# Idle matmuls, similarities and cluster rows moved in the prologue of a clustered-attention block on one Trainium2 core

## The chip, the cores and the metric

One NeuronCore of a Trainium2 chip runs the whole program. The metric is the device time of one execution in microseconds; several executions are timed and the median counts. One further execution is profiled.

The engines have these names in the rows: PE is TensorE (PEld its weight loads), DVE is VectorE, ACT is ScalarE, POOL is GpSimd, and SP is SyncE, whose queue issues every DMA of this kernel.

## What is computed

Batch 2, 8 heads, 768 positions, head size 64, 16 clusters per head. Queries and keys are put into the cluster whose centroid is most similar, a query sees only the keys of its own cluster, and two dense blocks follow.

```python
q_assign = np.argmax(np.einsum('bhsd,hcd->bhsc', q_n, c_n), axis=-1)
k_assign = np.argmax(np.einsum('bhsd,hcd->bhsc', k_n, c_n), axis=-1)
mask = q_assign[:, :, :, None] == k_assign[:, :, None, :]
scores = np.where(mask, scale * np.matmul(q, k.transpose(0, 1, 3, 2)), -1000000000.0)
scores = scores - np.max(scores, axis=-1, keepdims=True)
attn = np.exp(scores)
attn = attn / (np.sum(attn, axis=-1, keepdims=True) + 1e-09)
x = np.matmul(attn, v)          # then (B, S, H * D)
...
theta = x @ w_theta
y = w_tok_r @ (x * np.cos(theta)) + w_tok_i @ (x * np.sin(theta))
u = x + y
x = u + np.maximum(u @ w_ch, 0.0)
...
u = x + V.T @ (U.T @ x)
out = u + np.maximum(u @ w_ch1, 0.0) @ w_ch2
```

## The kernel before

**Tiles.** The 2 × 8 heads are worked on in eight pairs g = 0 to 7, two heads h per pair. A pair's queries and keys lie transposed, 128 × 768 (64 rows per head). For matmuls they are packed into tiles of 128 rows: `qp[s, h, w]` and `kp[s, h, w]`, in three sets s = g mod 3, with w = 0 and 1 for the high and the low parts of the numbers. Thirty-two of the 128 rows are free for extra terms: sixteen hold the **cluster rows**, a one-hot of the cluster on the query's side and 0 or -2**100 on the key's side, so that one matmul gives the score and its mask at once.

**Steps of a pair.**

- `split_hi`, `split_lo` (lines 186 to 194): hi on ACT, lo on POOL from the raw queries and keys; `pack` (line 215) copies them by DMA into the packed tiles.
- `assign_items` (line 115): the similarities `sims` on PE (line 121), then on DVE a transpose `s_t` (L124), the best similarity `mxc` (L128), four steps that make the one-hot `eqw` (L132 to L147) and a transpose back (L152).
- The cluster rows, in one of two ways. `mask_rows` (line 158): ACT makes `oh` (L161), and eight small DMAs copy it into the packed tiles. `mask_direct` (line 167): four matmuls turn the rows on PE (`oht`, L174), and ACT (L177, L179) or DVE (L181) copies them out. Pairs 0 and 1 use `mask_direct`, the later ones `mask_rows`.
- `max_pair(g, h, a)` (line 242): row maxima for two blocks of 128 queries, in three thirds of 512 columns, each with one bank `smax` (L251) and one reduction on DVE (L255). `max_join` joins the parts and splits them into two bf16 numbers, and `max_rows` (line 274) turns them into two more extra rows (`mrow`, L281; copied by ACT, L284).
- `scores_pair(g, h, a)` (line 294): transposed scores of two blocks of keys against all queries, in three thirds with one bank `st` each (L303); ACT takes the exp into `p` (L308).
- `pv` (line 312): products with V, four matmuls that the order lists and the trace book as eight, into two banks that are held until the pair's twelve are done; `sum_keys` (line 328): sums of the exps (`l`, L335).

**Order.** Nothing reorders the work: on every engine instructions run in the order of the code. PE's outputs go round a ring of eight banks of PSUM (`bank`, line 59), one of which, `hp`, is held for the idle matmuls of the prologue until its end (`give("hot")`). A step that needs a bank waits until the one before in it has been read.

The program has three parts. `prologue` (line 922) does the assignment and the cluster rows of pairs 0 and 1, all maxima of pair 0 and the scores of its head 0. `heat(n)` (line 927) issues n matmuls of a 128 × 512 tile of zeros whose result nobody reads. `attention` (line 829) loops over the pairs; in each of six places p it issues scores of pair g, then maxima of pair g + 1, then background work: `fill(t)` (line 811) takes items off the queue `bg` until their costs reach t, and conversions of weights when `bg` is empty. The splits of pair g + 2 and its one-hot steps stand in `bg`. PV products wait in `pvq` and are taken at p = 2 and p = 5. `mixer` (line 1016) is the rest.

SP's queue in the loop: at the start of pair g come V of pair g + 1, raw tiles of pair g + 3 and, from pair 1 on, weights; then the copies of `pack(g + 2)` as the splits come, then the eight copies of `mask_rows(g + 2)`.

Of the kernel before, what the change touches and what calls it, by code (L numbers as in the profile page):

```python
# [41 lines left out]
def tile_cluster_block(ctx: ExitStack, tc: tile.TileContext, qk, v, cent, wth, wr, wi, wch,  # L42
                       u_in, v_in, w1, w2, cst, out):
    nc = tc.nc
# [14 lines left out]
    def bank(name, keep=None):  # L59
        i = ring.popleft()  # L60
        if keep is None:
            ring.append(i)
        else:
            kept.setdefault(keep, []).append(i)
        return pp.tile([P, 512], F32, tag=f"bank{i}", name=name)
# [8 lines left out]
    def f32(ap):  # L74
        return ap.bitcast(F32)
# [91 lines left out]
    def mask_direct(g, h, eng):  # L167
        x = XROW[h]
        r = slice(x, x + 16)
        for i in range(2):  # L170
            for hf in range(2):
                o = 32 * (2 * i + hf) + 16 * h
                ps = bank("oht")
                nc.tensor.matmul(out=ps[r, :HALF], lhsT=identb[:, o:o + 16], rhs=onehots[g], start=True, stop=True)  # L174
                src, dst = ps[r, :HALF], (qp, kp)[i][g % SETS, h, 0][r, cols(hf)]
                if i == 0:
                    nc.scalar.activation(out=dst, in_=src, func=AF.Copy)  # L177
                elif eng is nc.scalar:
                    nc.scalar.activation(out=dst, in_=src, func=AF.Identity, scale=BIG, bias=kmul[r, 2:3])  # L179
                else:  # L180
                    eng.tensor_scalar(dst, src, BIG, BIG, op0=ALU.mult, op1=ALU.subtract)  # L181
# [9 lines left out]
    def split_lo(g, i, eng):  # L191
        t = slot(f"lo{g}_{i}", F32R)
        eng.tensor_tensor(t, raw[g, i], f32(hl[g, i, 0]), op=ALU.subtract)
        hl[g, i, 1] = t
# [44 lines left out]
    mx_t = {}  # L239
    THIRDS = [[(0, 0, 512)], [(0, 512, 256), (1, 0, 256)], [(1, 256, 512)]]  # L240

    def max_pair(g, h, a):

        s = g % SETS
        if a == 0:
            mx_t[g, h] = small.tile([P, 2 * NT], F32, tag="mx12", name="mx12")
        o = 2 * a
        for part in THIRDS:
            ps, c = bank("smax"), 0
            for j, k0, w in part:  # L250
                nc.tensor.matmul(out=ps[:, c:c + w], lhsT=qp[s, h, 0][:, (a + j) * P:(a + j + 1) * P],  # L251
                                 rhs=kp[s, h, 0][:, k0:k0 + w], start=True, stop=True)
                c += w
            n = len(part)
            nc.vector.tensor_reduce(mx_t[g, h][:, o:o + n], ps.rearrange("p (n w) -> p n w", n=n), axis=AX.X, op=ALU.max)  # L255
            o += n

    def max_join(g, h, act=False):
        mx = small.tile([P, NT], F32, tag="mx", name="mx")
# [34 lines left out]
    def scores_pair(g, h, a):  # L294

        s = g % SETS
        for kt in (a, a + 1):
            pt[g, h, kt] = slot(f"p{h}")
        for part in THIRDS:
            ps, c = bank("st"), 0  # L300
            for j, q0, n in part:
                for w in range(2):
                    nc.tensor.matmul(out=ps[:, c:c + n], lhsT=kp[s, h, w][:, (a + j) * P:(a + j + 1) * P],  # L303
                                     rhs=qp[s, h, w][:, q0:q0 + n], start=(w == 0), stop=(w == 1))
                c += n
            c = 0
            for j, q0, n in part:
                nc.scalar.activation(out=pt[g, h, a + j][:, q0:q0 + n], in_=ps[:, c:c + n], func=AF.Exp,  # L308
                                     scale=float(D) ** -0.5)
                c += n  # L310
# [496 lines left out]
    assign = {}  # L807
# [21 lines left out]
    def attention():  # L829


        ORDER = [(0, 0), (0, 2), (0, 4), (1, 0), (1, 2), (1, 4)]
        BURST = (2, 5)
        pvq = deque()
        held[0] = True

        def next_pv():
            g, kt, hf = pvq.popleft()
            pv(g, kt, hf)
            if kt == NT - 1 and hf:  # L840
                pv_out(g)

        for g in range(NG):
            nxt = g + 1 < NG
            if nxt:
                load_v(g + 1)
            if g + 2 < NG:
                bg.extend(split_items(g + 2, nc.gpsimd))
                bg.extend(assign.pop(g + 2))
            if g + 3 < NG:  # L850
                for i in range(2):
                    load_raw(g + 3, i)
            if g == 1:
                conv_load.extend(weigh_in(wth, NP * DM, wth_t))
                conv_start()
            if g == 2:
                tok = [c for p in zip(weigh_in(wr, NT * S, wr_t), weigh_in(wi, NT * S, wi_t)) for c in p]
                conv_load.extend(tok[:6])
                conv_start()
                late = tok[6:]  # L860
            if g == 6:
                conv_load.extend(late)
                conv_start()
            if not nxt:
                for t in range(NP):
                    bg.append((1., lambda t=t: split_x(0, t, nc.gpsimd)))
            order = [(1, 0), None, (1, 2), None, (1, 4), None] if g == 0 else ORDER
            for p in range(NT):
                ready = len(pvq)
                if order[p]:  # L870
                    h, a = order[p]
                    scores_pair(g, h, a)
                    if h:
                        pvq.extend((g, kt, hf) for kt in (a, a + 1) for hf in range(2))
                if g == 0 and p < 2:
                    mask_direct(1, p, nc.scalar if p else nc.vector)
                if nxt:
                    max_pair(g + 1, p // 3, 2 * p % 6)
                    if p % 3 == 2:
                        max_join(g + 1, p // 3)  # L880

                while conv_after:
                    conv_after.popleft()()
                if p == 3 and g + 2 < NG:
                    mask_rows(g + 2)
                if g > 0 and p == 5:
                    bg.appendleft((.95, lambda: norm_x(g - 1)))
                    bg.appendleft((.97, lambda: spread(g - 1)))
                fill(2. if not nxt else 4.8 if p in BURST else .3)
                if not nxt:  # L890
                    if p == 0:
                        sum_keys(g - 1, 1)
                    if p == 2:
                        max_rows(g, 1)
                    if p == 5:
                        sum_keys(g, 0)
                    for _ in range(min(ready, (2, 2, 2, 0, 4, 4)[p])):
                        next_pv()
                elif p in BURST:
                    if p == 2 and g > 0:  # L900
                        max_rows(g, 1)
                        sum_keys(g - 1, 1)
                    if p == 5:
                        max_rows(g + 1, 0)
                        sum_keys(g, 0)
                    for _ in range(min(ready, 6)):
                        next_pv()
                    if p == 5 and g + 3 < NG:
                        (_, sims), *assign[g + 3] = assign_items(g + 3)
                        sims()  # L910
                if g > 0 and p == 2:
                    row_sums(g - 1)
            while bg:
                fill(.5)
        held[0] = False
        while len(pvq) > 1:
            next_pv()
        nc.scalar.activation(out=warm, in_=warm, func=AF.Sin)
        next_pv()
        sum_keys(NG - 1, 1)  # L920

    def prologue():
# [4 lines left out]
        def heat(n):  # L927

            for _ in range(n):
                nc.tensor.matmul(out=hp, lhsT=hot[:, :P], rhs=hot[:, :512], start=True, stop=True)  # L930
# [34 lines left out]
        def run(items):  # L965
            for it in items:
                it[1]()

        its, its1 = assign_items(0), assign_items(1)
        for i in range(2):  # L970
            split_hi(0, i)
        split_lo(0, 0, nc.gpsimd)
# [8 lines left out]
        init_packs(1, nc.gpsimd)  # L981
        heat(14)
        run(its[1:])
        run(its1[:1])
        mask_direct(0, 0, nc.vector)
        mask_direct(0, 1, nc.scalar)
        split_lo(0, 1, nc.gpsimd)
        pack_low(0, (0, 1))
        for i in range(2):
# [2 lines left out]
        pack_direct(1, 0)  # L992
        pack(1, main=(1,))
        pack_low(1, (0,))
        for a in (0, 2, 4):
            max_pair(0, 0, a)
        max_join(0, 0, act=True)
        max_pair(0, 1, 0)
        max_pair(0, 1, 2)
        max_rows(0, 0)  # L1000
        init_packs(2, nc.gpsimd)
        scores_pair(0, 0, 0)
        max_pair(0, 1, 4)
        max_join(0, 1)
        run(its1[1:])
        scores_pair(0, 0, 2)
        heat(2)
        scores_pair(0, 0, 4)
        heat(2)
        max_rows(0, 1)  # L1010
        its2 = assign_items(2)
        run(its2[:4])
        assign[2] = its2[4:]
        give("hot")

    def mixer():
# [165 lines left out]
```

## Time and profile before

| what | value |
|---|---|
| median of 3 executions | 683.65 us (682.72 to 684.89) |
| the profiled execution | 684.69 us |
| its span, first to last instruction | 682.9 us |
| mean granted clock of TensorE | 0.994 |
| PE busy | 669.9 us, 98% of the span |
| DVE, ACT, POOL busy | 66%, 51%, 40% |

The span is what the profile shows; 1.8 us of the execution lie outside it. A busy time is the union of an engine's instructions, and a matmul is booked until its modelled end, so that PE's share holds more than the time in which it streams. The granted clock is the part of TensorE's full speed that the chip allows at the moment.

### The profile page before, as it was taken

To read this page: it belongs to the slowest core of one execution; us is meant where nothing else is said; L and a number is where in the kernel's file an instruction comes from. 1 tells how busy PE (TensorE), PEld (TensorE's weight loads), DVE (VectorE), ACT (ScalarE), POOL (GpSimd) and SP (SyncE) were. 2 spreads that over 40 slices of the span, in tenths; PEclk is the share of its full clock that TensorE was granted. 3 is DMA by queue.
4 is the path that set the end of the run, shared out by engine and by line. 5 is a ranking of instruction groups with operands and counts; after the bars stand their busy time and mean duration, and the time that the engine had idled before them with its cause. 6 is when DMAs were issued, how large, how long until landed. Compare 5 with 4: busy or idle time off the path is not lost.

```text
span 682.9 us, 11925 instructions
## 1 busy us (share of the span) xinstructions
PE 669.9 (98%) x4611; PEld 570.3 (84%) x4612; DVE 453.5 (66%) x800; ACT 350.5 (51%) x713; POOL 270.2 (40%) x273
## 2 busy tenths in 40 slices
PE   8999999999999999999999999999999999999997
PEld 3567766755765599999999998798899999999997
DVE  6887887898787367547375445877386766765554
ACT  7657656665776554456464344434454543543221
POOL 9423223133235324113223102466666566646221
PEclk9899999999999999999999999999999999999999
DMA  6768688576622102003110210212221212200013
GB/s 206 206 146 254 167 239 230 158 195 159 178 94 87 54 1 78 1 1 108 47 42 12 78 32 1 79 61 78 76 78 56 71 61 78 63 0 1 1 47 138
DMA packets 21784, 62.55 MB, mean 92 GB/s; under 512 B 4224, under 2 KB 7296, under 8 KB 21728
## 3 DMA queue, kind: packets, MB, share of 16 engines
q1 hardware_dynamic: 21728, 61.80, 30.9%
q8 instruction: 36, 0.59, 0.3%
q14 instruction: 20, 0.16, 0.1%
HBM read 40.35 MB, written 3.15 MB: 64 GB/s over the span
## 4 chain that ended last, share of the span: by engine, by line
PE 89%; DVE 6%; ACT 4%; issue 1%; DMA 0%; SPq 0%; DVEq 0%; ACTq 0%
PE y L562 15%; PE acc L796 15%; PE q L744 13%; PE pv L316 9%; PE st L303 8%; PE l L335 5%; PE th L520 5%; PE acc L717 5%; PE g L698 4%; PE h L582 4%; PE smax L251 3%; DVE mx L255 2%; ACT p L308 2%; PE sims L121 1%; DVE xT L646 1%; ACT hi L188 1%
## 5 line engine op out<-in xcount | busy, mean ns | idle before, releaser
L255 DVE TENSOR_REDUCE mx<-smax 128x1 f32<-128x512 f32 x144 | 89.6, 682 | 21.9 <-PE smax L251 21.9
L401 POOL TENSOR_TENSOR wl<-cv,wh 128x768 fp32r<-128x768 f32 (+1 forms) x33 | 57.9, 1754 | 115.2 <-ACT wh L397 93.7
L308 ACT ACTIVATE p<-st 128x512 f32<-128x512 f32 x192 | 79.0, 513 | 44.2 <-PE st L303 43.3
L796 PE MATMUL acc<-g,wh 128*128 128x384 f32 x384 | 97.5, 334 | 0.0
L562 PE MATMUL y<-wh,z 128*128 128x384 f32 x384 | 87.6, 340 | 0.3 <-ACT z L540 0.3
L758 POOL TENSOR_TENSOR g<-sum,g 128x384 fp32r<-128x384 f32 x48 | 53.3, 1113 | 80.7 <-ACT g L757 75.5
L752 DVE TENSOR_TENSOR xT<-acc,xT 128x384 f32<-128x384 f32 x96 | 53.3, 556 | 45.0 <-PE acc L796 44.8
L303 PE MATMUL st<-qp,kp 128*128 128x256 f32 (+1 forms) x384 | 79.4, 349 | 0.4 <-ACT qp L284 0.2
L303 PEld LDWEIGHTS st<-qp,kp 128*128 128x128 f32 x384 | 58.3, 192 | 18.9 <-issue 8.5
L796 PEld LDWEIGHTS acc<-g,wh 128*128 128x128 f32 x384 | 69.3, 188 | 0.0
L562 PEld LDWEIGHTS y<-wh,z 128*128 128x128 f32 x384 | 66.9, 188 | 0.5 <-ACT z L540 0.5
L316 PE MATMUL pv<-p,v 128*32 128x384 f32 x768 | 66.2, 486 | 0.0
L796 PE MATMUL acc<-g,wl 128*128 128x384 f32 x192 | 64.1, 334 | 0.0
L752 DVE TENSOR_TENSOR sum<-q,sum 128x384 f32<-128x384 f32 x84 | 45.5, 554 | 27.2 <-PE q L744 22.0
L756 ACT ACTIVATE sum<-sum 128x384 f32<-128x384 f32 x48 | 25.1, 523 | 67.5 <-DVE sum L752 67.5
L316 PEld LDWEIGHTS pv<-p,v 128*32 128x32 f32 x768 | 31.6, 110 | 29.4 <-issue 20.7
L546 POOL TENSOR_TENSOR z<-tht,z 128x256 fp32r<-128x256 f32 x24 | 19.3, 802 | 87.6 <-ACT z L540 87.5
L392 DVE SCALAR_TENSOR_TENSOR cv<-cv,st 128x768 int32<-128x768 int32 (+3 forms) x47 | 46.8, 995 | 3.1 <-ACT cv L385 2.6
L562 PE MATMUL y<-wl,z 128*128 128x384 f32 x192 | 48.8, 335 | 0.0
L251 PE MATMUL smax<-kp,qp 128*128 128x512 f32 x192 | 44.2, 349 | 3.0 <-ACT qp L177 1.9
L251 PEld LDWEIGHTS smax<-kp,qp 128*128 128x128 f32 x192 | 33.0, 191 | 12.7 <-issue 2.9
L385 ACT ACTIVATE cv<-st 128x768 f32<-128x768 f32 (+3 forms) x47 | 38.3, 815 | 10.3 <-POOL wl L401 4.1
(170 smaller groups left out, 1450.7 us busy)
## 6 DMA issues: line engine op xcount, KB each, us to landing
st<-in_w_dram SPq DMA_DIRECT2D x17, 512.0 KB, 3.4
st<-in_w_dram SPq DMA_DIRECT2D x10, 768.0 KB, 4.1
raw<-in_qk_dram SPq DMA_DIRECT2D x16, 384.0 KB, 4.5
qp<-hi SPq DMA_DIRECT2D x26, 192.0 KB, 2.9
st<-in_wr_dram SPq DMA_DIRECT2D x6, 768.0 KB, 4.6
st<-in_wi_dram SPq DMA_DIRECT2D x6, 768.0 KB, 4.3
kp<-hi SPq DMA_DIRECT2D x32, 96.0 KB, 3.1
qp<-lo SPq DMA_DIRECT2D x32, 96.0 KB, 2.7
```

What stands on the lines that cost most here:

```text
L251: nc.tensor.matmul(out=ps[:, c:c + w], lhsT=qp[s, h, 0][:, (a + j) * P:(a + j + 1) * P], rhs=kp[s, h, 0][:, k0:k0 + w], start=True, stop=True)
L255: nc.vector.tensor_reduce(mx_t[g, h][:, o:o + n], ps.rearrange("p (n w) -> p n w", n=n), axis=AX.X, op=ALU.max)
L303: nc.tensor.matmul(out=ps[:, c:c + n], lhsT=kp[s, h, w][:, (a + j) * P:(a + j + 1) * P], rhs=qp[s, h, w][:, q0:q0 + n], start=(w == 0), st ...
L308: nc.scalar.activation(out=pt[g, h, a + j][:, q0:q0 + n], in_=ps[:, c:c + n], func=AF.Exp, scale=float(D) ** -0.5)
L316: nc.tensor.matmul(out=pvt[g][hf][r:r + 32, :HALF], lhsT=v_t[g][:, kt, r:r + 32], rhs=pt[g, r // 64, kt][:, cols(hf)], start=(kt == 0), st ...
L392: nc.vector.scalar_tensor_tensor(t, t, 3, self.lw, op0=ALU.logical_shift_left, op1=ALU.bitwise_or)
L401: nc.gpsimd.tensor_tensor(t[:, :c.w], c.t, f32(c.hi[:, :c.w]), op=ALU.subtract)
L562: nc.tensor.matmul(out=yps[u, j][hf][:, :HALF], lhsT=lhs, rhs=w[st][e][:, hf * HALF:(hf + 1) * HALF], start=(st == 0 and n == 0), stop=(st ...
L744: nc.tensor.matmul(out=ps[:, :HALF], lhsT=w[a][:, j * P:(j + 1) * P], rhs=u_block(self.b, y, e, j), start=(n == 0), stop=(n == 5))
L752: nc.vector.tensor_tensor(out, ps[:, :HALF], x, op=ALU.add)
L758: nc.gpsimd.tensor_tensor(t[:, 1], r, f32(t[:, 0]), op=ALU.subtract)
L796: nc.tensor.matmul(out=ps[:, :HALF], lhsT=wv[a], rhs=self.g[i, hf][:, x], start=(m == 0), stop=(m == 5))
```

## The change

In the prologue: idle matmuls are added (three behind pair 0's cluster rows, one behind each third of four of pair 0's six groups of maxima, six before pair 1's first cluster rows) and two times two are removed. The similarities of pair 1 move from before pair 0's cluster rows to behind its first group of maxima, with `s_t` and `mxc`. The similarities of pair 2 move ahead of `max_rows(0, 1)`, and its step L132 moves out of the prologue into the background of the loop. Pair 1's cluster rows move from the loop into the prologue, one head before and one behind the scores (0, 1, 0), which come with them.

In the loop: pair 0's remaining scores are issued at p = 1 and p = 3, its first four PV products stand in the queue from the start, and at p = 5 of pair 0 four instead of six are taken.

```diff
-    def max_pair(g, h, a):
+    def max_pair(g, h, a, warmer=None):
...
             nc.vector.tensor_reduce(mx_t[g, h][:, o:o + n], ps.rearrange("p (n w) -> p n w", n=n), axis=AX.X, op=ALU.max)
             o += n
+            if warmer:
+                warmer(1)
...
-        pvq = deque()
+        pvq = deque((0, kt, hf) for kt in (0, 1) for hf in range(2))
...
-            order = [(1, 0), None, (1, 2), None, (1, 4), None] if g == 0 else ORDER
+            order = [None, (1, 2), None, (1, 4), None, None] if g == 0 else ORDER
...
-                if g == 0 and p < 2:
-                    mask_direct(1, p, nc.scalar if p else nc.vector)
...
-                    for _ in range(min(ready, 6)):
+                    for _ in range(min(ready, 6 if g else 4)):
...
-        its, its1 = assign_items(0), assign_items(1)
+        its, its1, its2 = assign_items(0), assign_items(1), assign_items(2)
...
         run(its[1:])
-        run(its1[:1])
         mask_direct(0, 0, nc.vector)
         mask_direct(0, 1, nc.scalar)
+        heat(3)
...
-        for a in (0, 2, 4):
-            max_pair(0, 0, a)
+        max_pair(0, 0, 0)
+        run(its1[:2])
+        max_pair(0, 0, 2, heat)
+        max_pair(0, 0, 4, heat)
         max_join(0, 0, act=True)
-        max_pair(0, 1, 0)
-        max_pair(0, 1, 2)
+        max_pair(0, 1, 0, heat)
+        max_pair(0, 1, 2, heat)
         max_rows(0, 0)
         init_packs(2, nc.gpsimd)
         scores_pair(0, 0, 0)
         max_pair(0, 1, 4)
         max_join(0, 1)
-        run(its1[1:])
+        run(its1[2:])
         scores_pair(0, 0, 2)
-        heat(2)
         scores_pair(0, 0, 4)
-        heat(2)
+        run(its2[:2])
         max_rows(0, 1)
-        its2 = assign_items(2)
-        run(its2[:4])
-        assign[2] = its2[4:]
+        heat(6)
+        mask_direct(1, 0, nc.vector)
+        scores_pair(0, 1, 0)
+        mask_direct(1, 1, nc.scalar)
+        assign[2] = its2[3:]
         give("hot")
```

**Around the first maxima.** DVE before, from the transpose of pair 0's one-hot (`eqw`) on; `kp_87` is the key tile of set 0, head 0, w = 0:

```order
L152 STREAM_TRANSPOSE eqw<-eqw 128x384
L124 STREAM_TRANSPOSE s_t<-sims 128x384
L181 TENSOR_SCALAR kp_87<-oht 16x384 x2
L255 TENSOR_REDUCE mx_288<-smax 128x1
L255 TENSOR_REDUCE mx_288<-smax 128x2
```

and DVE now:

```order
L152 STREAM_TRANSPOSE eqw<-eqw 128x384
L181 TENSOR_SCALAR kp_87<-oht 16x384 x2
L255 TENSOR_REDUCE mx_284<-smax 128x1
L255 TENSOR_REDUCE mx_284<-smax 128x2
L255 TENSOR_REDUCE mx_284<-smax 128x1
L124 STREAM_TRANSPOSE s_t<-sims 128x384
L128 TENSOR_REDUCE mxc<-s_t 128x24
L255 TENSOR_REDUCE mx_284<-smax 128x1
```

Pair 1's `s_t` went from ahead of the cluster-row copy to behind the first three reductions, and `mxc`, which stood behind all of pair 0's maxima, came along. PE now, in the same place (`raw_0_120` and `raw_1_122` are pair 1's raw tiles, `qp_85` is the query tile beside `kp_87`):

```order
L251 MATMUL smax<-kp_87,qp_85 128x512
L121 MATMUL sims<-raw_0_120,cblk 32x384
L121 MATMUL sims<-raw_1_122,cblk 32x384
L121 MATMUL sims<-raw_0_120,cblk 32x384
L121 MATMUL sims<-raw_1_122,cblk 32x384
L251 MATMUL smax<-kp_87,qp_85 128x512
L930 LDWEIGHTS hot
L930 MATMUL hot<-hot 128x512
L251 MATMUL smax<-kp_87,qp_85 128x256 x2
L930 LDWEIGHTS hot
L930 MATMUL hot<-hot 128x512
```

Before, the maxima stood there one behind the other.

**At the end of the prologue, on ACT.** `p` are exps, `qp_93` belongs to pair 1's head 0, `qp_97` and `kp_99` to its head 1, `hi_0` and `hi_1` are the splits of pair 2. Before:

```order
L308 ACTIVATE p_468<-st 128x512
L177 ACTIVATE qp_93<-oht 16x384 x2
L188 ACTIVATE hi_0_507<-raw_0_194 128x768
L188 ACTIVATE hi_1_509<-raw_1_196 128x768
L177 ACTIVATE qp_97<-oht 16x384 x2
L179 ACTIVATE kp_99<-oht,kmul 16x384 x2
L308 ACTIVATE p_556<-st 128x512
```

Now:

```order
L310 ACTIVATE p_489<-st 128x512
L177 ACTIVATE qp_97<-oht 16x384 x2
L179 ACTIVATE kp_99<-oht,kmul 16x384 x2
L188 ACTIVATE hi_0_534<-raw_0_194 128x768
L188 ACTIVATE hi_1_536<-raw_1_196 128x768
L310 ACTIVATE p_560<-st 128x512
```

The copies of head 1's cluster rows went ahead of the splits (those of head 0 now stand ahead of the exps `p_488` and `p_489`).

**In the loop, on ACT.** Pair 2, first half, from the conversion `wh` behind the first exps on; `hi_0`, `hi_1` are the splits of pair 4. Before:

```order
L397 ACTIVATE wh<-cv 128x768
L308 ACTIVATE p_1109<-st 128x512
L308 ACTIVATE p_1109<-st 128x256
L308 ACTIVATE p_1110<-st 128x256
L308 ACTIVATE p_1110<-st 128x512
L188 ACTIVATE hi_0_1136<-raw_0_728 128x768
L188 ACTIVATE hi_1_1138<-raw_1_730 128x768
L308 ACTIVATE p_1162<-st 128x512
```

Now:

```order
L310 ACTIVATE p_1153<-st 128x512
L310 ACTIVATE p_1153<-st 128x256
L310 ACTIVATE p_1154<-st 128x256
L310 ACTIVATE p_1154<-st 128x512
L188 ACTIVATE hi_0_1185<-raw_0_737 128x768
L188 ACTIVATE hi_1_1187<-raw_1_739 128x768
L286 ACTIVATE qp_106<-mrow 2x384 x2
```

The splits went from between the second and the third exps to behind the third. The same holds for pair 3; in pair 1 they went from behind the first exps to behind the third, and in pairs 4 and 5 from between the second and third to directly behind `wh`, ahead of the second.

## Rows read from the trace of the kernel before

**Rows 1.** The page, section 2: granted clock in 40 equal slices of the span.

```profile
PEclk9899999999999999999999999999999999999999
```

**Rows 2.** Busy time of each engine by stretch; then granted clock, DMA share, GB/s.

```profile
core 0: us, PE busy (x) PEld busy (x) DVE busy (x) ACT busy (x) POOL busy (x), PEclk, DMA share, GB/s
14.53:21.22 6.69, 5.63 (x21) 3.26 (x21) 5.87 (x12) 4.99 (x9) 5.95 (x5) 0.91 0.88 273
21.22:26.80 5.58, 5.29 (x20) 3.92 (x20) 4.58 (x8) 2.82 (x6) 4.44 (x7) 0.50 0.96 207
...
33.17:37.63 4.46, 3.26 (x17) 1.75 (x16) 3.00 (x7) 4.39 (x10) 1.77 (x1) 1.00 0.16 36
```

**Rows 3.** Timeline, 10 to 40 us, all engines: start, length, engine, what, count, wait before.

```profile
9.67 2.14 PE L930 MATMUL hot<-hot 128*128 128x512 bf16 x9
...
11.07 0.58 DVE L152 STREAM_TRANSPOSE eqw<-eqw 128x384 bf16<-128x384 bf16 x1
...
12.66 0.58 DVE L124 STREAM_TRANSPOSE s_t<-sims 128x384 f32<-128x384 f32 x1 [1.02 <-PE sims L121]
...
13.28 1.04 DVE L181 TENSOR_SCALAR kp<-oht 16x384 fp32r<-16x384 f32 x2
...
14.53 6.24 PE L251 MATMUL smax<-kp,qp 128*128 128x512 f32 x20 [0.74 <-ACT qp L177]
...
15.04 5.47 DVE L255 TENSOR_REDUCE mx<-smax 128x1 f32<-128x512 f32 x9 [0.72 <-PE smax L251]
...
21.22 0.49 PE L281 MATMUL mrow<-identb,m 128*2 128x128 bf16 x6 [0.45 <-DVE m L271]
...
26.37 1.76 PE L303 MATMUL st<-qp,kp 128*128 128x512 f32 x8
...
30.92 0.58 DVE L152 STREAM_TRANSPOSE eqw<-eqw 128x384 bf16<-128x384 bf16 x1
...
33.17 0.82 PE L174 MATMUL oht<-eqw,identb 128*16 128x384 bf16 x4
...
34.88 1.58 ACT L188 ACTIVATE hi<-raw 128x768 fp32r<-128x768 f32 x2
...
35.18 0.93 PE L251 MATMUL smax<-kp,qp 128*128 128x512 f32 x4 [1.20 <-ACT qp L177]
...
35.85 3.74 POOL L193 TENSOR_TENSOR lo<-raw,hi 128x768 fp32r<-128x768 f32 x2 [10.14 <-issue]
```

**Rows 4.** Timeline of PE alone, 27 to 53.4 us.

```profile
39.91 2.79 PE L316 MATMUL pv<-p,v 128*32 128x384 f32 x32
...
53.31 0.50 PE L303 MATMUL st<-qp,kp 128*128 128x512 f32 x1
```

**Rows 5.** Timeline of SP's queue, 53.9 to 80 us: start and length of the issues.

```profile
54.00 1.38 SPq L376 DMA_DIRECT2D st<-in_wth_dram  x3
...
67.81 0.54 SPq L213 DMA_DIRECT2D qp<-lo  x1
...
76.61 0.54 SPq L213 DMA_DIRECT2D kp<-oh  x1
```

**Rows 6.** DMA issues, 53.9 to 79.7 us: count, KB each, median us to landing.

```profile
st<-in_wth_dram SPq DMA_DIRECT2D x1, 512.0 KB, 12.8
...
kp<-oh SPq DMA_DIRECT2D x4, 24.0 KB, 1.9
```

**Rows 7.** Timeline of PE alone, 77.2 to 90.6 us.

```profile
78.82 0.86 PE L251 MATMUL smax<-kp,qp 128*128 128x512 f32 x4
...
83.01 0.85 PE L251 MATMUL smax<-kp,qp 128*128 128x512 f32 x4
...
84.51 2.14 PE L335 MATMUL l<-p,ones 128*32 128x384 f32 x24 [0.21 <-ACT p L308]
```

**Rows 8.** Timeline of ACT alone, 77.2 to 90.6 us.

```profile
81.79 1.64 ACT L188 ACTIVATE hi<-raw 128x768 fp32r<-128x768 f32 x2
...
83.26 1.69 ACT L308 ACTIVATE p<-st 128x512 f32<-128x512 f32 x4
```

## The prediction

> **What bounds the kernel now.** I read the granted clock first, then the prologue in order of time on all engines, then PE through the loop of pair 0, then the DMA queue, and last one later pair on PE and ACT. TensorE is the engine that sets the time, and nearly the only stretch in which it neither works densely nor runs at full speed is the prologue. The clock line shows one loss: of its forty digits the second is 8, and all others are 9 [rows 1]. The stretches show where: 0.91 of full clock while the first maxima are taken (14.53 to 21.22 us), 0.50 in the 5.58 us behind them, 1.00 again later [rows 2]. 0.50 is the lower of TensorE's two levels, 1.2 GHz. In the stretch ahead of the fall PE is booked 5.63 of 6.69 us, but that is 20 matmuls of the maxima and little else; it is DVE that works through, one third of a pair of row maxima every 0.6 us (9 in 5.47 us) [rows 3]. So PE waits for banks there and the matmuls come in small groups.
>
> The other idle place is the wait for the second pair's cluster rows: the maxima at 35.18 wait 1.20 us, and PE is busy only 3.26 of the 4.46 us around it [rows 2, 3].
>
> **The change, part by part.** Each step is dated against the profiled execution.
>
> *Similarities of pair 1 out of the way.* Their transpose s_t stands on DVE at 12.66 to 13.24, ahead of the cluster-row copy kp at 13.28 (1.04 us for two) [rows 3]. Without sims and s_t the turned rows can follow eqw (ready at 11.65) directly: cluster matmuls at 11.7, kp copied by about 13.35, first maxima at 13.55 in place of 14.53. The three idle matmuls put in here cost nothing as long as they stay under that copy; at 0.24 us each (9 in 2.14 us) [rows 3] they end at about 13.55 too. If the copy came earlier they would be the wait. Gain 0.95.
>
> *It comes back on DVE.* The first nine reductions now have s_t and mxc among them, 0.6 us each. Ready for mrow: 13.55 + 0.5 + 9 × 0.6 + 1.2 + 0.8 for joining and splitting, about 21.45, against 21.22 [rows 3]: 0.25 later. So the first scores start no earlier.
>
> *The idle matmuls.* Twelve of 0.24 us are put where PE waits for DVE: per third 0.24 of maxima and 0.24 idle work against DVE's 0.6. They fit; what they are for is the clock. Taken as held at 1.00, the scores and maxima from 21.45 on run at full rate; the next limit is DVE's reductions, which release the banks. The second scores pair then starts at about 25.3 in place of 26.37 [rows 3]. Gain 1.1.
>
> The Trainium skill, page "TensorE: Matmul & The Clock Gate", section "Why this matters for your kernels", says that what drops the clock in mid-kernel is idle gaps between bursts of matmuls, and means gaps far longer than any in this stretch; by that rule the clock would not have fallen here, and more matmuls could not mend it. The row on the clock says that it fell, so the row decides here; what the rule would give is rival 2.
>
> *Cluster rows of pair 1 before head 1's scores.* DVE ends the chain of pair 1 at about 30.05 in place of 31.50, six idle matmuls end at about 30.3 (0.2 us too late, the one place where they cost), cluster rows, scores (0,1,0) and the other cluster rows follow without a gap, and pair 1's maxima start at about 33.05 instead of 35.18 [rows 3], with four cluster matmuls already done (0.8 us of PE as in the row at 33.17).
>
> *The loop of pair 0.* It took from 35.18 to 53.31 [rows 3, 4] with PE dense. It loses one scores pair and the cluster rows to the prologue and passes 16 of its PV matmuls (half of the 32 at 39.91 in 2.79 us [rows 4], so 1.35 us) on to pair 1. But it is now thin on PE and meets two others. ACT: the two splits hi (1.58 us [rows 3]) stand behind all four cluster copies and ahead of the exps of scores (0,1,2), whose banks the third maxima and the PV products need. From 35.0 the splits run to 36.5, the first bank is read at 37.15 and the last at 38.1; PE would want them 0.6 and 0.3 us before: 0.9 of waiting. DVE: 14 of the 18 reductions must be done before `l` gets a bank. From 33.55 these are 14 × 0.6 us, and the five steps of pair 2's one-hot (some 0.55 each, as L152 [rows 3]) with a join stand among them, 3.4 us: 45.4, where PE could be 1.2 us before. Behind it come 2.0 for `l`, 2.6 for four PV products and 0.65 for sims: 50.6 for the first scores of pair 1, 2.7 earlier, and 1.35 of it is owed later. Net 1.35, and nearly 1.7 at the first scores of pair 2, since ACT no longer splits between two exps of pair 1.
>
> *Where that ends.* The first maxima of pair 3 (78.82 [rows 7]) need four small copies of cluster rows, the last issued at 76.61 on SP [rows 5] and landing 1.9 us later [rows 6], at 78.5. That is 0.3 us ahead of PE. SP issues in order: behind the weight loads (issued 54.00 to 55.38) its copies stop until the third weight load lands (12.8 us after issue [rows 6], so 67.8), and from 67.81 on it issues without a break, twenty copies of some 0.6 us [rows 5]. Backwards this hangs on the split of pair 2, hi at 34.88 on ACT and lo at 35.85 on POOL (3.74 us) [rows 3]. The change puts cluster copies ahead of hi and brings all else forward; I get 34.9 to 35.05, no earlier. So SP's queue is not moved, PE may run 1.7 us ahead and waits for 78.5 to 78.7. What is left of the gain is 0.1 us (bounds: none of it, if hi is a little later; all of 1.7, if the copies did not decide).
>
> *The shifted background.* Because pair 2's one-hot has a step more to do in the loop, the splits of later pairs move on ACT. In pairs 2 and 3 they stood between the second and third exps (hi at 81.79, p at 83.26 [rows 8]) and made l at 84.51 wait [rows 7]; now they come behind. Worth 0.2 (the wait that the row names) to 0.8 (84.51 less the end of a 0.7 us group begun at 83.01 [rows 7]); I take 0.55 each, because mrow stands between the two and takes a part of the larger. In pairs 4 and 5 they come ahead of the second exps, where the scores of the third pair then wait for banks: 0 to 1.6 us lost, the whole 1.64 of the two splits; I take 0.4 each, since PE's two groups take 2.1 us (78.82 to 83.01 is two pairs) against ACT's 1.69 [rows 7, 8], which gives back 0.4 a time, and part of the wait was there before. Later pairs and the conversions behind only change places; I put 0 ± 0.5 on them.
>
> The sum: 0.1 + 2 × 0.55 − 2 × 0.4 = 0.4 us saved. The profiled execution took 684.69, its span 682.9 and 1.8 around it, 1.0 more than the median of 683.65; the sum makes 684.3 of it, and by the same difference **683.2** of the median.
>
> **The rivals.** About 0.3% (2.05 us) is what a measurement of this kernel can tell from no change.
>
> 1. *The copies do not decide* (SP comes earlier, or the reshuffled background gains in more places than it loses). Then the 1.7 us stay, with 1.1 from pairs 2 and 3, less 0.8: 681.6; without the loss in pairs 4 and 5, 680.8. For it: the slack is a few tenths of a microsecond, and such an issue row varies by that. Against it: twenty issues in a row without a gap. 0.22.
>
> 2. *The idle matmuls do not hold the clock.* PE then meets 21.45 to 27 at half rate as now, 0.25 later than now and with the extra matmuls in the way, hi comes about 1.1 later, and the copies with it: 0.8 lost at pair 3, 0.3 won behind: 684.1. For it: the page's rule above; against it: PE will be issuing in every gap. 0.10.
>
> 3. *The clock falls in the new wait*, at the first maxima of pair 3. PE arrives some 1.6 us early and stands still at a place where it is the bound from then on. The fall in the prologue lasted at least the 5.58 us of [rows 2] at half rate, which in a dense stretch is 2.8 us of work: 686.1. It decides from a wait longer than any that the clock has survived so far, 1.20 us at 35.18 [rows 3]. Against it: PE was dense on both sides of that one, as it is here. 0.07.
>
> 4. *The splits of pair 2 come late.* Each microsecond by which hi starts behind 35.2 moves the copies of pair 3 by as much. From about 2.3 us on the kernel is slower by more than can be told from nothing: 685.8. 0.07, since what ACT waits for ahead of that place comes 2 us forward.
>
> My forecast has 0.54; its own range is 682.2 to 684.4.
>
> **How the numbers follow.** Of rival 1 some two thirds lie over 0.3%, and a little of the forecast's reordering: faster 0.18. Rivals 3 and 4 make slower 0.14. The rest is within 0.3%: 0.68. The range of 681.0 to 685.2 holds the forecast, rival 2 and most of rival 1, and leaves out rivals 3 and 4.
>
> **What would show it.** Right: granted clock 1.00 from 13 to 30 us; first maxima near 13.6 but mrow still near 21.4; pair 1's maxima near 33; first scores of pair 1 near 50.6; the split hi of pair 2 near 35; and the first maxima of pair 3 at 78.5 to 78.7, waiting for a DMA, with l of pair 2 behind it near 83.9. Wrong: those maxima starting near 77 (rival 1), a digit under 9 in the clock line (2 or 3), or hi of pair 2 behind 36 (4).

## The result and the profile after

The changed kernel takes **688.52 us** (median of 6 executions, 688.03 to 689.49) against 683.66 (682.72 to 684.89, 6 executions beside it). The ratio is 1.0070, with a 95% interval of 1.0057 to 1.0082: 4.8 us slower, where 683.2 was forecast. The profiled execution took 688.61 us, its span is 686.8. All six executions have a mean granted clock of 0.998, as the profiled one has. Line numbers behind L257 are those of the kernel before plus 2.

First the page's clock line of the kernel after, then its busy times by stretch (columns as in [rows 2]).

```profile
PEclk9999999999999999999999999999999999999999
```

```profile
21.17:27.98 6.81, 6.14 (x34) 4.35 (x34) 6.66 (x14) 4.83 (x12) 3.81 (x6) 1.00 0.98 207
35.64:41.87 6.23, 6.07 (x50) 3.44 (x49) 6.20 (x10) 3.10 (x8) 3.82 (x2) 1.00 0.70 158
41.87:46.51 4.64, 3.05 (x14) 1.85 (x13) 4.50 (x11) 1.66 (x4) 0.00 (x0) 1.00 0.84 190
46.51:50.48 3.97, 3.82 (x30) 1.26 (x33) 3.45 (x8) 0.96 (x2) 0.00 (x0) 0.57 0.67 147
```

The fall behind the first maxima is gone: 1.00 where [rows 2] have 0.50. But there is a new one, too short for a digit of the page: 0.57 in the stretch at 46.51, behind a stretch in which PE was booked 3.05 of 4.64 us. The timeline of PE through the loop of pair 0 shows both (columns as in [rows 3]):

```profile
37.62 2.79 PE L318 MATMUL pv<-p,v 128*32 128x384 f32 x32
40.34 1.68 PE L305 MATMUL st<-qp,kp 128*128 128x512 f32 x8
41.87 1.55 PE L251 MATMUL smax<-kp,qp 128*128 128x512 f32 x8
44.72 1.70 PE L251 MATMUL smax<-kp,qp 128*128 128x512 f32 x4 [1.30 <-DVE mx L255]
46.51 0.45 PE L283 MATMUL mrow<-identb,m 128*2 128x128 bf16 x6
47.10 3.55 PE L337 MATMUL l<-p,ones 128*32 128x384 f32 x24
...
53.81 0.50 PE L305 MATMUL st<-qp,kp 128*128 128x512 f32 x1
```

PE waits 1.30 us for a reduction, and `l`, which takes 2.14 us at full rate [rows 7], takes 3.55. The first scores of pair 1 come at 53.81; 50.6 was forecast, 53.31 stands in [rows 4]. What DVE did, in the timeline of all engines at 38 us, and then of DVE alone:

```profile
37.97 1.83 POOL L193 TENSOR_TENSOR lo<-raw,hi 128x768 fp32r<-128x768 f32 x1
38.03 1.98 DVE L138 TENSOR_TENSOR eqw<-eqw,cvals 128x384 bf16<-128x384 bf16 x1
```

```profile
36.23 1.88 DVE L255 TENSOR_REDUCE mx<-smax 128x1 f32<-128x512 f32 x3
...
39.93 1.87 DVE L255 TENSOR_REDUCE mx<-smax 128x1 f32<-128x512 f32 x3
```

L138 is the weigh step of pair 2's one-hot, 0.36 us elsewhere. It came 0.06 us behind the start of the second split `lo` on POOL and ended only after it (39.80), 1.6 us late. In the profile of before the same step came in the last moment of the first `lo`:

```profile
37.50 0.39 DVE L138 TENSOR_TENSOR eqw<-eqw,cvals 128x384 bf16<-128x384 bf16 x1
```

The other new loss is in pair 1. POOL, DVE and PE of the kernel after, around 62 us:

```profile
61.20 1.83 POOL L193 TENSOR_TENSOR lo<-raw,hi 128x768 fp32r<-128x768 f32 x1 [21.41 <-ACT hi L188]
62.99 1.83 POOL L193 TENSOR_TENSOR lo<-raw,hi 128x768 fp32r<-128x768 f32 x1
```

```profile
61.85 0.17 DVE L262 TENSOR_REDUCE mx<-mx 128x6 f32<-128x12 f32 x1
62.05 1.02 DVE L272 CAST m<-mx 128x6 bf16<-128x6 f32 x1
63.10 1.74 DVE L273 TENSOR_TENSOR m<-mx,m 128x6 bf16<-128x6 f32 x1
```

```profile
68.60 0.50 PE L251 MATMUL smax<-kp,qp 128*128 128x512 f32 x1 [1.41 <-DVE lt L340]
```

Two tiny steps that split the maxima take 1.02 and 1.74 us in place of 0.18 and 0.17, each until a `lo` has ended. All of DVE's one-hot work is pushed behind them, and PE waits 1.41 us for a bank. The same two stalls stand in pairs 2 and 3 (at 88.2 and 114.3), where before only the cast was late, by 0.53 and 0.38. In pair 1 the splits came two scores pairs earlier before, and met no such step.

**A mechanism that the forecast lacked.** Steps of DVE that read two operands from SBUF (L138, L273) or cast from SBUF to SBUF (L272) wait for the end of the `lo` that POOL is running. Reductions do not: three from PSUM (L255, 1.88 us in all) ran beside the first `lo` of pair 2, and one from SBUF (L262) took 0.17 us at 61.85 beside the `lo` that began at 61.20. The Trainium skill states this, page "SBUF — State Buffer", section "Who interferes with whom": DVE and GpSimd share one pair of ports under an exclusive lock, the one that starts first keeps it for its whole instruction, and reductions don't take it. The rows above agree.

### The profile page after: what moved, and what is told of

Read it like the earlier page. It is cut to its first block, busy times and chain, and to the rows that moved or that the text cites. A ratio compares the mean times of both kernels' runs of the same rounds, so it can differ in the third digit from the quotient of the medians.

```text
span 686.8 us, 11962 instructions
## 1 busy us (share of the span) xinstructions
PE 671.3 (98%) x4627; PEld 577.2 (84%) x4629; DVE 459.9 (67%) x800; ACT 351.3 (51%) x713; POOL 269.2 (39%) x273
## 4 chain that ended last, share of the span: by engine, by line
PE 83%; DVE 9%; ACT 4%; DMA 2%; SPq 1%; issue 1%; ACTq 0%; DVEq 0%
PE y L564 15%; PE acc L798 15%; PE q L746 13%; PE st L305 7%; PE pv L318 7%; PE th L522 5%; PE acc L719 5%; PE g L700 4%; PE l L337 4%; PE h L584 4%; DVE mx L255 4%; PE smax L251 3%; DMA raw<-in_qk_dram 1%; ACT p L310 1%; DVE xT L648 1%; PE tp L602 1%
## 5 line engine op out<-in xcount | busy, mean ns | idle before, releaser
L255 DVE TENSOR_REDUCE mx<-smax 128x1 f32<-128x512 f32 x144 | 89.7, 682 | 21.5 <-PE smax L251 21.5
L305 PE MATMUL st<-qp,kp 128*128 128x256 f32 (+1 forms) x384 | 78.0, 345 | 2.4 <-ACT p L310 1.4
L305 PEld LDWEIGHTS st<-qp,kp 128*128 128x128 f32 x384 | 56.9, 188 | 21.5 <-issue 5.3
L318 PEld LDWEIGHTS pv<-p,v 128*32 128x32 f32 x768 | 37.4, 110 | 23.8 <-issue 8.2
L251 PE MATMUL smax<-kp,qp 128*128 128x512 f32 x192 | 46.0, 355 | 4.4 <-DVE lt L340 2.0
L394 DVE SCALAR_TENSOR_TENSOR cv<-cv,st 128x768 int32<-128x768 int32 (+3 forms) x47 | 45.4, 967 | 1.7 <-ACT cv L387 1.3
L193 POOL TENSOR_TENSOR lo<-raw,hi 128x768 fp32r<-128x768 f32 x16 | 29.2, 1843 | 37.7 <-ACT hi L188 26.7
```

The lines of the kernel that those rows point to most:

```text
L318: nc.tensor.matmul(out=pvt[g][hf][r:r + 32, :HALF], lhsT=v_t[g][:, kt, r:r + 32], rhs=pt[g, r // 64, kt][:, cols(hf)], start=(kt == 0), st ...
L394: nc.vector.scalar_tensor_tensor(t, t, 3, self.lw, op0=ALU.logical_shift_left, op1=ALU.bitwise_or)
```

## The experiments

Each run was timed in five rounds; ratios are against executions of the kernel before on the same chip, and are not the quotients of the medians quoted. A loss in us is the ratio less 1, times 683.6.

**1. The background's balance.** The order of background items hangs on `owed`, the balance that `fill` carries along. Pair 2's extra step leaves it 0.56 lower at the end of pair 0, and so every later split waits for a larger `fill`.

```diff
         for g in range(NG):
             nxt = g + 1 < NG
+            if g == 1:
+                owed[0] += 0.56
```

> The changed kernel with the background's balance put back by 0.56 at the start of pair 1, so that from pair 1 on every background step stands where it stands in the kernel before; prologue and loop of pair 0 as changed. Theory A (the shifted background costs: the splits lo on POOL now fall on the steps on DVE that split the maxima, which take 1.0 and 1.7 us in place of 0.18 there): from pair 1 on the changed kernel lost 3.4 us against before, 1.35 of it owed products, so 2.0 come back: 686.5 us, and those two steps take 0.18 us again in pairs 1 to 3. Theory B (as predicted, the shift itself gains a little, and all is lost in pair 0): 688.5 to 689.0 us.

Measured: 686.17 us, ratio 1.0038 [1.0025, 1.0052]. The steps are short again, in pair 1:

```profile
62.27 0.18 DVE L272 CAST m<-mx 128x6 bf16<-128x6 f32 x1
62.48 0.17 DVE L273 TENSOR_TENSOR m<-mx,m 128x6 bf16<-128x6 f32 x1
```

The shift costs 4.8 − 2.6 = 2.2 us here. The stalls of pair 1 are only a part of that. Set beside the profile of this run, the first row sums `l` of a pair come 1.45 us late in pair 1 of the change, 1.6 in pair 3, 1.7 in pair 5 and 3.0 in pair 7. So the stalls of pairs 2 and 3 delay PE hardly further, and the other half comes late, where no split is left but the conversions of weights have changed places too. One of these meets POOL in pair 6, ahead of the reductions:

```profile
188.90 1.85 POOL L403 TENSOR_TENSOR wl<-cv,wh 128x768 fp32r<-128x768 f32 x1 [13.85 <-ACT wh L399]
189.36 2.20 DVE L394 SCALAR_TENSOR_TENSOR cv<-cv,st 128x768 int32<-128x768 int32 x1
192.22 1.69 PE L251 MATMUL smax<-kp,qp 128*128 128x512 f32 x4 [0.36 <-DVE mx L255]
```

L394 takes 0.96 us where it meets no POOL instruction. It also meets one in the run with the balance put back, at 200.2 us (2.21), so how much of the late half is its doing was not tested.

And the other way round, in the kernel before, with `-= 0.56` (written as `+= -0.56`):

> The kernel before with the background's balance lowered by 0.56 at the start of pair 1, and nothing else: the shifted background alone. Theory A (the shift costs 2.0): 685.7 us, with the two steps that split the maxima at 1.0 and 1.7 us in pairs 1 to 3. Theory B (the shift gains 0.3): 683.4 us.

Measured: 688.27 us, ratio 1.0068 [1.0051, 1.0085]; 4.6 us, more than expected. Waits of PE, 50 to 135 us (what waited for what, us, times, longest), PE's timeline, and the stretches:

```profile
PE smax L251 <- DVE lt L338: 3.3, 2, 2.8
```

```profile
66.77 0.79 PE L251 MATMUL smax<-kp,qp 128*128 128x512 f32 x1 [2.76 <-DVE lt L338]
67.36 2.67 PE L303 MATMUL st<-qp,kp 128*128 128x512 f32 x8
```

```profile
62.00:66.40 4.40, 2.01 (x11) 1.59 (x11) 4.17 (x8) 2.43 (x7) 0.93 (x1) 1.00 1.03 211
66.40:69.80 3.40, 3.04 (x9) 2.65 (x10) 2.45 (x6) 1.68 (x4) 1.49 (x8) 0.50 0.97 218
```

One number in a balance costs as much as the whole change: DVE's stall makes PE wait 2.76 us, and the clock falls behind it. In the changed kernel the 1.35 us of PV products passed on from pair 0 fill a part of that wait (1.41 us are left, and the clock reads 1.00 behind them), which fits that the shift costs less there.

**2. The profile of before was an unlucky one.** Of 80 executions of the kernel before that were timed beside these experiments the median is 683.6 us, and 20 took 684.6 or more, as the profiled one did (684.69). Up to pair 1 the last kernel is the kernel before, yet its profile is 1.4 us ahead. PE's timeline of the kernel before, then of this run:

```profile
6.12 1.51 PE L121 MATMUL sims<-raw,cblk 128*32 128x384 f32 x8 [0.55 <-DVE cblk L963]
7.57 4.25 PE L930 MATMUL hot<-hot 128*128 128x512 bf16 x14
11.74 0.85 PE L121 MATMUL sims<-raw,cblk 128*32 128x384 f32 x8
```

```profile
6.12 0.89 PE L121 MATMUL sims<-raw,cblk 128*32 128x384 f32 x8 [0.69 <-DVE cblk L965]
6.94 3.19 PE L932 MATMUL hot<-hot 128*128 128x512 bf16 x14
10.06 0.85 PE L121 MATMUL sims<-raw,cblk 128*32 128x384 f32 x8
```

Fourteen idle matmuls take 4.25 us in the one and 3.19 in the other: in the profile of before TensorE still ran at its lower level until 9.7 us, here until 4.9. (This is read from the idle matmuls, which are booked 0.63 us at the lower level and 0.38 at the full one; the clock column reads 1.00 in both.) So pair 1's similarities came at 11.74 and kept `s_t` in the way; with the clock up early they come at 10.06, `s_t` is done before the cluster-row copies need DVE, and the first maxima start at 13.08. The Trainium skill says that the moment of this rise differs between runs of one kernel (page "TensorE: Matmul & The Clock Gate", section "Part 1: The HAM clock gate"); these rows agree. Step one of the forecast, 0.95 us, was read from that execution.

**3. The idle matmuls of the prologue.** The change without the twelve (`max_pair(0, 0, 2)` for `max_pair(0, 0, 2, heat)` and so on):

> The changed kernel without the twelve idle matmuls among the first maxima. Theory A (they hold TensorE's clock there, and pair 0 passes about half of that on): the clock reads 0.5 for some 7 us from about 20 us on, the first maxima of pair 1 come at 34.4 in place of 33.4, and the time is 689.0 us. Rival (idle matmuls only take PE's time, or the clock would have held without them): 1.0 throughout, 688.5 us or less.

Measured: 689.39 us, ratio 1.0084 [1.0066, 1.0102], against 1.0070 of the change: not told apart. In the profile the clock falls in the prologue (0.72 from 21 to 27 us) and holds at 47, though PE waits there as in the change:

```profile
45.49 1.69 PE L251 MATMUL smax<-kp,qp 128*128 128x512 f32 x4 [1.33 <-DVE mx L255]
```

```profile
47.30:51.00 3.70, 3.44 (x46) 1.47 (x49) 3.60 (x9) 0.96 (x2) 0.00 (x0) 1.00 0.63 140
```

In three of the six executions the mean clock is 0.998 (687.83 to 689.02 us), in the other three 0.993 to 0.995 (689.75 to 690.52). Alone, in the kernel before (with the `warmer` of the change):

> The kernel before with the twelve idle matmuls among the first maxima, and nothing else. Theory A (they hold the clock): 1.0 in place of 0.5 from 18 to 26 us, second scores pair some 4.0 us behind the first rows of maxima in place of 5.2, 682.0 us. Rival (DVE's reductions set the pace there, or what is gained is waited for at the cluster rows of pair 1): 683.1 us, as before.

Measured: 683.55 us, ratio 0.9991 [0.9978, 1.0004]. The clock holds, 1.00 from 13 to 28 us in the profile and 1.00 on the mean in all twelve executions, and the second scores come 3.9 us behind the first rows of maxima in place of 5.2 [rows 3], but the time is not told from before. Its twelve executions lie in two groups, five from 681.76 to 681.97 and seven from 683.52 to 683.95; the profiled one is of the upper group, and its first idle matmuls run at the lower level as in the profile of before (14 in 4.64 us). With the similarities moved as in the change:

```diff
-        run(its1[:1])
...
         max_pair(0, 0, 0)
+        run(its1[:2])
...
-        run(its1[1:])
+        run(its1[2:])
```

> The last one, and the similarities of pair 1 moved behind the first third of the maxima as in the change. Theory A (in an execution whose clock is up early the similarities were hidden under the last one-hot step, so that the move only puts two more steps among DVE's reductions): first maxima no earlier, first rows of maxima 1.1 us later than in the last one, 683.1 us. Rival (as predicted, first maxima 0.95 us earlier): the rows 0.2 us later at most, 682.0 us or less.

Measured: 682.99 us, ratio 0.9999 [0.9987, 1.0010]. The move gains nothing. From the first maxima to the first `mrow` it now takes 8.9 us (13.60 to 22.54) against 6.7 in the last run: `s_t` and `mxc` are 1.1 of it (in the change, whose clock held, the same way takes 7.8), and beside the rest stands a fall of the clock (the similarities at 14.61 take 1.51 us) that this execution had and the other had not.

**4. The loop of pair 0.** Clock alone: an idle matmul into the bank that each third of head 1's maxima overwrites next.

```diff
+    hotw, WARM = [], (0, 1)
...
             ps, c = bank("smax"), 0
+            if g == 1:
+                for _ in range(WARM[h]):
+                    nc.tensor.matmul(out=ps, lhsT=hotw[0][:, :P], rhs=hotw[0][:, :512], start=True, stop=True)
...
         nc.vector.memset(hot[:, :512], 0.0)
+        hotw.append(hot)
```

> The changed kernel with one idle matmul of 0.24 us ahead of each third of head 1's maxima in the loop of pair 0 (9 in all), into the bank that the third then overwrites. Theory A (the clock fell at 46.6 us because PE only waits for reductions there, and row sums and products at half rate cost 1.6 us): clock 1.0 from 6 us on, row sums in 2.0 in place of 3.6 us, 686.9 us. Rival (the fall is not from these waits, or the idle matmuls take as much as they save): 688.5 us or more.

Measured: 687.13 us, ratio 1.0054 [1.0041, 1.0068]. The first scores of pair 1 come at 52.34, 1.5 us earlier, and the clock holds:

```profile
41.00:46.40 5.40, 5.40 (x28) 3.18 (x27) 5.23 (x13) 2.35 (x5) 0.00 (x0) 1.00 0.82 186
46.40:50.40 4.00, 3.74 (x51) 1.63 (x54) 3.90 (x9) 0.96 (x2) 0.00 (x0) 1.00 0.71 156
```

With the balance put back as well:

> The changed kernel with the balance put back, and one idle matmul ahead of each third of head 1's maxima in the loop of pair 0: the clock alone. Theory A (the fall costs 1.4 to 1.6 us by itself): 684.7 us. Rival (without the shift it is absorbed behind): 686.2 us.

Measured: 684.16 us, ratio 1.0009 [1.0000, 1.0017]. Its weigh step still takes 1.97 us. The stall alone, with the balance put back in the same way, by moving the second split:

```diff
-                bg.extend(split_items(g + 2, nc.gpsimd))
-                bg.extend(assign.pop(g + 2))
+                sp_, as_ = split_items(g + 2, nc.gpsimd), assign.pop(g + 2)
+                if g:
+                    bg.extend(sp_ + as_)
+                else:
+                    bg.extend([sp_[0], sp_[2], *as_[:2], sp_[1], sp_[3], *as_[2:]])
```

> The changed kernel with the balance put back from pair 1 on, and in pair 0 the second split hi of pair 2 (and with it the second lo on POOL) issued behind the weigh step in place of ahead of it; DVE's work is the same. Theory A (the weigh step waits for the POOL instruction that runs when it comes, and that wait is a loss of its own): it finds POOL between its two splits and takes 0.36 us in place of 1.97, row sums of pair 0 start 1.6 us earlier (45.2 in place of 46.8), 684.6 us, or 683.0 if the clock then holds. Rival (DVE's load, not that wait, delays the row sums): weigh short, row sums near 46.5, 686 us.

Measured: 684.33 us (683.17 to 687.89), ratio 1.0013 [1.0000, 1.0027]. DVE's weigh step, and PE's clock in the stretch of the row sums:

```profile
37.82 0.34 DVE L138 TENSOR_TENSOR eqw<-eqw,cvals 128x384 bf16<-128x384 bf16 x1
```

```profile
45.00:49.00 4.00, 3.74 (x49) 1.59 (x52) 3.60 (x9) 0.96 (x2) 0.00 (x0) 1.00 0.97 210
```

With the stall goes the fall of the clock (the mean clock is 0.999 or 1.00 in eleven of the twelve executions), and `l` starts at 45.3. The stall mended in another way, by taking compare and weigh into the prologue (the balance, 0.44 lower by this order, put back by as much), first without the idle matmuls, then with them, which is both mendings together:

```diff
-        assign[2] = its2[3:]
+        run(its2[3:5])
+        assign[2] = [PAUSE] + its2[5:]
```

> The changed kernel with the background's balance put back from pair 1 on, and with the second and third step of pair 2's one-hot (compare, weigh: 0.92 us on DVE) done at the end of the prologue, where DVE waits, instead of in the loop of pair 0. Theory A (the weigh step, which waited 1.6 us for the split lo on POOL, and DVE's load were what delayed pair 0): row sums of pair 0 near 44.5 us in place of 46.8, and 684.0 us, or 682.4 if TensorE's clock then holds too. Rival (the loop waits for PE or ACT anyway): row sums at 46 or later and 686.2 us as with the balance alone.

Measured: 684.10 us, ratio 1.0006 [0.9996, 1.0016].

> The last one, and one idle matmul ahead of each third of head 1's maxima in the loop of pair 0. Theory A (stall, clock and shift are the three losses, and they add up): clock 1.0 from 6 us on, 682.5 us, so no slower than the kernel before. Rival (the change as such, four PV products late and the scores early, costs): 684 us or more.

Measured: 683.58 us, ratio 1.0008 [1.0000, 1.0017]. So stall and clock don't add up: either mending alone, and both, end within 1.0006 to 1.0013, about 2 us under the balance alone (1.0038), and the 683.0 and 682.4 us expected for a mended stall with the clock held did not come. The run that keeps the stall and loses only the fall (1.0009) is no slower than the one that loses both (1.0013): with the clock held, the stall costs nothing that shows. What a shorter loop gains beyond the 2 us is given back within two pairs. PE in the run with the two steps in the prologue:

```profile
47.12 2.76 PE L318 MATMUL pv<-p,v 128*32 128x384 f32 x32
...
50.46 1.66 PE L305 MATMUL st<-qp,kp 128*128 128x512 f32 x8
```

```profile
77.88 0.94 PE L251 MATMUL smax<-kp,qp 128*128 128x512 f32 x4 [0.70 <-DMA kp<-oh]
```

Pair 1 starts at 50.46, and PE waits at pair 3's first maxima for the copies of cluster rows. In the run with the second split moved, which starts pair 1 as early, it waits 0.7 us for ACT's copy of the maxima rows in place of that.

**5. A version that beats both.** The kernel before with the twelve idle matmuls, and one more in the gap ahead of the first similarities; and the mended change with that one:

```diff
         nc.tensor.transpose(ct[:, :P], cdup.rearrange("p a d -> p (a d)"), ident)
+        heat(1)
```

> The kernel before with the twelve idle matmuls, and one more behind the very first transpose, where TensorE stands still for 0.55 us between it and the first similarities. Theory A (executions whose clock rises at 4 to 6 us are about 1.5 us faster than those whose clock rises at 10, and that gap decides which it is): the clock rises before 7 us, all runs near 681.8 us. Rival (the moment of the rise doesn't hang on the gap): two groups of runs, near 681.8 and 683.6, as without it.

Measured: **681.89 us** (nine executions, 681.70 to 683.08), ratio **0.9970** [0.9960, 0.9980]. None of the nine lies in the upper of the two groups. The run without the extra idle matmul was timed on another chip only, so that a difference between chips is not ruled out. In the profile the clock is up before 7 us:

```profile
6.91 3.20 PE L932 MATMUL hot<-hot 128*128 128x512 bf16 x14
...
13.06 1.64 PE L251 MATMUL smax<-kp,qp 128*128 128x512 f32 x7 [0.58 <-ACT qp L177]
```

> The changed kernel with the balance put back, compare and weigh done in the prologue, and the same one idle matmul behind the first transpose: the change without its three losses. Theory A: 683.5 us, no faster than before, since what the prologue gains goes into the PV products passed on. Rival (early rise is what it lacked): 682.3 us or less.

Measured: 683.53 us, ratio 0.9996 [0.9987, 1.0006]. The kernel before comes to the time of the best one by itself, but seldom: 4 of its 80 executions have a mean clock of 1.00 and took 681.74 to 681.86 us, the other 76 have 0.994 to 0.997 and took 682.69 to 685.43. Without its losses the change is even with the kernel before, and slower than idle matmuls alone. PE of the best kernel at the end of pair 0 says why:

```profile
45.71 4.12 PE L318 MATMUL pv<-p,v 128*32 128x384 f32 x48
49.58 0.89 PE L121 MATMUL sims<-raw,cblk 128*32 128x384 f32 x8
50.41 1.66 PE L305 MATMUL st<-qp,kp 128*128 128x512 f32 x8
```

It reaches pair 1 at 50.41, as the mended change does at 50.46, with 48 products done at that place in place of 32. Scores and cluster rows that are brought forward relieve the loop on PE alone. As far as the profile shows, DVE's reductions then set its length (`l` waits 0.26 us for one), and what is left of the gain are sixteen products that still have to be done.

## Why the prediction was wrong, step by step

- **Similarities out of the way, 0.95 us: wrong.** First maxima at 13.40, as forecast (13.55), but the comparison was with a profiled execution whose clock rose late; the same program otherwise reaches them at 13.08. The working treated that execution's extra 1.0 us as an offset that lay nowhere. It lay in the very stretch that the change touches.
- **It comes back on DVE: right.** `mrow` at 21.17 (forecast 21.45).
- **The idle matmuls hold the clock: right** (1.00 to 46 us), second scores at 25.09 (25.3). Their worth, 1.1 us there, was not told from nothing in the time by itself; rival 2 fell with it. The page's rule weighed there (the Trainium skill, page "TensorE: Matmul & The Clock Gate", section "Why this matters for your kernels": what drops the clock are far longer gaps) is not borne out either: the clock fell again behind a longest wait of 1.30 us.
- **Pair 1's maxima near 33.05: right** (33.42).
- **The loop of pair 0, first scores of pair 1 at 50.6: the step that failed first.** Its sum is right where the weigh step meets a free POOL: `l` at 45.3 and scores at 50.56 in the run that moves the second split, 45.4 and 50.6 forecast. In the change it waited 1.6 us for POOL, PE thinned out and `l` began 1.8 us later (47.10), the clock fell, and from there the way to pair 1 took 1.4 us more: 53.81. The forecast counted what DVE does but not whom its steps meet, and had the fall of the clock as a rival only at pair 3.
- **The cap at pair 3's cluster rows: right where PE comes early.** The wait for these copies ends at 77.88 in the run with two steps in the prologue (78.5 to 78.7 forecast). In the change PE is late, and pair 3's first maxima start at 81.45 without a wait.
- **The shifted background, 0.3 gained: the step that cost most, and of the wrong sign.** The splits did leave the place between the exps (the row sums of pairs 2 and 3, with `mrow`, take 2.02 us in place of 2.51, so 0.5 of the 0.55 forecast is there), but they took their `lo` onto the two steps that split the maxima. Measured 2.2 us lost in the change, 4.6 in the kernel before.
- **Pairs 4 and 5, 0.8 lost: right in kind, too large.** The third scores wait there, 0.69 us at 137.79 and 0.66 at 164.59, but the lag behind the run with the balance put back only grows from 1.6 to 1.7 us. **Later pairs, 0 ± 0.5: wrong**; that lag, read from one profile of each, grows by 1.3 us more up to pair 7.

By the runs the 4.8 us are 2.2 of shift and about 2 of stall and clock in pair 0 (one loss, since either mending removes it). The parts depend on the order in which they are taken: with the clock held first (1.0070 to 1.0054) that is 1.1 us and the shift 3.1; the sum, 3.9 to 4.4, hardly does. What is left, 0.4 to 0.9 us, is hardly told from nothing, and lies near the even result that the forecast had for a change without these two. Rival 1 fell too: the copies don't decide in the change, and it is slower. Rival 3 has the kind of loss right, a clock that falls behind a new wait longer than 1.20 us (1.30), but put it at pair 3 and not in pair 0's loop; and the length of a wait does not decide it, since the clock held behind 1.41 us in pair 1 of the same profile and behind 1.33 in the run without the twelve. Rival 4 did not come: hi of pair 2 starts at 35.01, as forecast.

Left open: what the fall of the clock would cost without the stall, since no run had that; what decides whether it falls; where the late half of the shift's cost comes from; and in how many executions of each kernel the clock rises late, since one of each was profiled and the mean clock does not show it (it is 1.00 in both groups of the kernel before with the twelve).

## What to carry to other kernels

When a change shifts a queue of background work, go through every engine pair that runs at the new times: a two-operand or casting step on DVE can last until the POOL instruction that it meets has ended, however small it is. Compare profiled executions of the same program before reading a gain of a microsecond from the start of one; where the clock rises at different moments, an idle matmul in the gap ahead of it is worth a try, and here went with more than the reordering gained. Work moved into idle time on one engine is worth little if the stretch it leaves is bound by another.

## What was not expected of the hardware

- The order of 0.06 us decides over 1.6: the weigh step at 38.03 behind a `lo` that began at 37.97 took 1.98 us; in the profile of before, at 37.50 ahead of one, 0.39.
- TensorE's clock fell behind stretches with PE booked 3.05 of 4.64 us (longest wait 1.30) and 2.01 of 4.40 (2.76), and held where idle matmuls filled the former: booked 5.40 of 5.40. It also held behind a wait of 1.33 us without them, so these figures are no rule.
- One idle matmul in a gap of 0.55 us ahead of the first similarities went with nine executions within 1.4 us and none near 683.6, where seven of twelve lay without it, on another chip.
